# Token-list rows of 64 bytes, and the transposes of the third unit of 256 tokens two parts later in TensorE's order

## The chip, the cores and the metric

The kernel runs on one core of one Trainium2 chip. Its engines are TensorE (PE, with its weight loads shown apart as PEld), VectorE (DVE), ScalarE (ACT), GpSimd (POOL) and SyncE (SP), and 16 DMA engines serve the core. POOL and SP issue DMAs: SP's go out on the queue that the trace calls hardware_dynamic, POOL's indirect ones on software_dynamic. The metric is device time in microseconds, the median of several executions. One further execution was profiled, and all rows of the trace come from that one.

## What is computed

Three stages follow one another on 2 x 768 tokens of 512 values in float32.

```
x   = attention(q, k, v) with a mask: query and key in the same nearest-centroid cluster
e   = argmax(x @ w_gate + bias[modality]);  g = softmax weight of expert e
y   = g * (relu(x @ w1[e]) @ w2[e])            # one of 8 experts per token
h   = y @ w_in;  out = (max(h,0) + log1p(exp(-|h|))) @ w_out
```

The expert stage is the one of interest: each token goes to one of eight experts, so tokens have to be sorted by expert, gathered, multiplied by that expert's weights, and put back.

## The kernel before, in words

**Stages.** Attention of batch 0, then of batch 1 (to about 300 us), the experts, and the dense pair of matmuls at the end. The work of the expert stage starts for batch 0 while attention of batch 1 still runs. The order in which the code issues instructions is the order on each engine: there is a manual schedule and no scheduler behind it. DMAs of SP and POOL also go out in the order of the code on these engines.

**The token list.** After routing, each token has a row number in a list in device memory, `token_list`: 1536 rows per expert and some rows for surplus, 13312 rows in all. `scatter_list` (L592 to 599, the DMA is issued on L589) writes the tokens' numbers into it: for each batch six indirect DMAs of 128 rows, issued by POOL, with a small memset `spacer` (L588) ahead of each. A row is one 4-byte word. `init_list` fills the list once, early in attention: POOL sets the tile `empty` (L1035), and SP stores it. The tokens' own rows `x_rows` (2 KB each) are stored apart.

**Units.** Tokens are worked on in units. F0 and F1 are full units of 256 tokens of batch 0, chosen early. F2 to F4 are full units whose expert and place in the list come from tables made once all tokens are routed; M1 to M3 are small units (32, 128 and 32 tokens); F5 is a late one. For a unit of the tables
- `u_list` (L752 to 766): SP reads the place from a register load (L757) and loads the token numbers, `it<-token_list` (L765 or L762),
- `u_gather` (L768 to 779): POOL clips them (`gi`, L772) and gathers the rows of x by them, one indirect DMA per 128 tokens (`xg<-x_rows,gi`, L776),
- `u_xpose` (L793 to 798, with `to_T`): PE transposes 128 tokens in four matmuls into the one PSUM bank `misc` (L785), ACT copies them to `xh` (L788), and DVE subtracts to get the low half `xl` (L790),
- `l1_part` (L818) multiplies by the first weights in four groups for each half of the hidden values, s=0 and s=1, and `l2_part` (L843) by the second: for each half 24 matmuls, 12 into the bank of j=0 and 12 into that of j=1,
- `u_out` copies and scatters the result, `y_rows<-ysb,it`.

**Weights.** They come as chunks of 512 KB: SP loads `raw` (L730), ACT casts the high half `wh` (L740), and DVE or POOL subtracts the low half `wl` (L741). A matmul group takes `wh`, `wl` and `wh` again.

**The order.** A list `seq` of parts (unit, layer, half) sets what PE does. Tables made ahead of it say what is issued with each part: `before` (the transposes ahead of a part), `gathers`, `loads`, `todo` (the splits). F2 and M1 are the first two units that take their places from the tables: both list loads and all three gathers of these two are issued with the last layer-1 part of F1, behind the list's second six scatters. On POOL the subtraction of one weight chunk, wl_3783, stands behind the three gathers. It is the low half of F1's first chunk of second weights, so it belongs to the second matmul of F1's layer 2.

Of the kernel before, what the change touches and what calls it, by code (L numbers as in the profile page):

```python
# [12 lines left out]
U32 = mybir.dt.uint32  # L13
# [19 lines left out]
def body(ctx, tc, qT, kT, vP, cen, mod, wg, bias, w1, w2, win, wout, out):  # L33
    nc = tc.nc
# [4 lines left out]
    NT = S // 128  # L39
# [2 lines left out]
    DUMMY = E * CAP  # L42
    LATE = DUMMY + 256 * NF
    LROWS = LATE + 256
    NM = N // 256
    CW = 1024
    pe, dve, act, pool, sp = nc.tensor, nc.vector, nc.scalar, nc.gpsimd, nc.sync

    xd = nc.dram_tensor("x_rows", (N, DM), F32, kind="Internal").ap()
    yd = nc.dram_tensor("y_rows", (N, DM), F32, kind="Internal").ap()  # L50
    lst = nc.dram_tensor("token_list", (LROWS, 1), U32, kind="Internal").ap()
    wf = nc.dram_tensor("w_rows", (16, 128, 1024), F32, kind="Internal").ap()

    const = ctx.enter_context(tc.tile_pool(name="const", bufs=1))
# [10 lines left out]
    def ctile(shape, dt, name):  # L65
        return const.tile(shape, dt, name=name)
# [2 lines left out]
    desc8 = ctile([128, E], F32, "desc8")  # L69
    tri = ctile([128, 128], BF16, "tri")  # L70
    ones = ctile([128, 128], BF16, "ones")
    tokid = ctile([128, 2 * NT], U32, "tokid")
    gate = ctile([128, 2 * NT], F32, "gate")
    lbias = ctile([128, 2 * NT, E], F32, "lbias")
    lacc = [ctile([128, NT, E], F32, f"lacc{b}") for b in range(2)]
# [29 lines left out]
    def setup_late():  # L105
        pool.iota(desc8, pattern=[[-1, E]], base=E, channel_multiplier=0, allow_small_or_imprecise_dtypes=True)
        pool.iota(e_off, pattern=[[CAP, E]], base=0, channel_multiplier=0, allow_small_or_imprecise_dtypes=True)
        pool.iota(tokid, pattern=[[128, 2 * NT]], base=0, channel_multiplier=1)
        pool.memset(e_row, 0.0)
        pool.iota(e_row[0:1], pattern=[[0, NT + 1], [CAP, E]], base=0, channel_multiplier=0, allow_small_or_imprecise_dtypes=True)  # L110
        pool.memset(e_row[0:1, NT, :], 0.0)
        pool.iota(iota_u, pattern=[[1, 16]], base=0, channel_multiplier=0, allow_small_or_imprecise_dtypes=True)
        pool.iota(u_fix, pattern=[[0, 3], [1, NK]], base=0, channel_multiplier=0, allow_small_or_imprecise_dtypes=True)
        for i, b in enumerate((128, 32, 0)):
            pool.iota(thr[:, i, :], pattern=[[256, 6]], base=b, channel_multiplier=0, allow_small_or_imprecise_dtypes=True)
        dve.tensor_reduce(out=fold, in_=ident.rearrange("p (g t) -> p t g", g=4), axis=AX.X, op=ALU.add)
        pool.iota(x_row, pattern=[[CAP, 9]], base=0, channel_multiplier=0, allow_small_or_imprecise_dtypes=True)
        pool.memset(ones, 1.0)
        pool.memset(tri, 1.0)
        pool.affine_select(  # L120
            out=tri, in_=tri, pattern=[[1, 128]], base=0, channel_multiplier=-1,
            compare_op=ALU.is_gt, fill=0.0,
        )
        pool.memset(pre9, 1.0)
        pool.affine_select(
            out=pre9, in_=pre9, pattern=[[1, 9], [-1, E]], base=0, channel_multiplier=0,
            compare_op=ALU.is_gt, fill=0.0,
        )
        pool.memset(drow, 0.0)
        pool.memset(nunit, 0.0)  # L130
        pool.memset(d_row, 0.0)
# [462 lines left out]
    def scatter_list(b, idx):  # L594
        for t in range(NT):
            scatter(
                "list", out=lst, out_offset=bass.IndirectOffsetOnAxis(ap=idx[:, t:t + 1], axis=0),
                in_=tokid[:, b * NT + t:b * NT + t + 1], in_offset=None,
            )

    def pick_early(cnt):
# [152 lines left out]
    def u_list(u, eng=sp):  # L754
        b = u["base"]
        if not isinstance(b, int):
            b = eng.value_load(b, min_val=0, max_val=DUMMY + 256 * (NF - 1))  # L757
        it = small.tile([128, 2], U32, tag="it", name="it", bufs=NF + NHU + NTU + 3)
        gi = small.tile([128, 2], U32, tag="gi", name="gi", bufs=NF + NHU + NTU + 3)
        with nc.allow_non_contiguous_dma(reason="token lists are columns of words"):  # L760
            if u["tiny"]:
                eng.dma_start(out=it[:32, 0:1], in_=lst[bass.ds(b, 32)])  # L762
            else:
                n = u["n"]
                eng.dma_start(out=it[:, :n], in_=lst[bass.ds(b, 128 * n)].rearrange("(j p) o -> p (j o)", p=128))  # L765
        u["it"], u["gi"] = it, gi

    def u_gather(u):  # L768
# [23 lines left out]
    def u_xpose(u, j):  # L792
        if j == 0:  # L793
            w = 32 if u["tiny"] else 128 * u["n"]
            u["xh"] = u["xtp"].tile([128, 4, w], F32 if u["tiny"] else F32R, tag="xh", name="xh")
            u["xl"] = None if u["tiny"] else u["xtp"].tile([128, 4, w], F32R, tag="xl", name="xl")
        to_T(u["xg"][j], u["xh"], u["xl"], j, 32 if u["tiny"] else 128)
# [47 lines left out]
    def u_out(u, j, free=True):  # L845
        y = u["yp"].tile([128, DM], F32, tag="ysb", name="ysb")
        if j == 0:
            act.copy(y, u["y"][j])
        else:
            dve.tensor_copy(y, u["y"][j])  # L850
        kw = dict(
            out=yd, out_offset=bass.IndirectOffsetOnAxis(ap=u["it"][:, j:j + 1], axis=0),
            in_=y, in_offset=None, bounds_check=N - 1, oob_is_err=False,
        )
        if free:
            scatter("late" if u["late"] else "y", **kw)
        else:
            pool.indirect_dma_start(**kw)
# [85 lines left out]
    with tc.manual_schedule():  # L944
# [83 lines left out]
                    busy.add(g0 + k)  # L1028
            after.setdefault(g0 + 4, []).append((cv_store, (j,)))

        e_t = p_1.tile([128, LROWS // 128], U32, name="empty")

        def init_list():
            setup_late()
# [235 lines left out]
        def at_part(table, n, x):  # L1270
            table.setdefault(n, []).append(x)

        for (kd, k, layer, s), n in pos.items():
            if layer == 1 and s == 0 and n > 1:
                v = (F if kd == "F" else M)[k]
                back = [x for x in range(2, n) if seq[x][0] == "F" or seq[x][2] < 3]
                for j in range(v["n"]):
                    at_part(before, back[j - v["n"]], (v, j))
                if v not in early_ and v is not U1:
                    at_part(gathers, [x for x in back if seq[x][0] == "F"][-3 if kd == "F" else -4], v)  # L1280
        nsplit = [0]
# [132 lines left out]
        for n in range(2, end):  # L1414
            kind, i, layer, s = seq[n]
            if n == x_at:
                extra_units()
            u = (F if kind == "F" else M)[i]
            if n == x_at + 2:
                for k in range(3):  # L1420
                    y_load(k)
                y_gate(0)
                y_gate(1)

            for v, j in before.get(n, ()):
                u_xpose(v, j)
            if kind == "F" and layer == 1:
                for f in range(4):
                    l1_part(u, s, f)
            elif kind == "F" and i == LF:  # L1430
                if s == 0:
                    for j in range(2):
                        l2_part(u, 0, [j])
                        if j:
                            y_T(0, 1)
                        l2_part(u, 1, [j])
                        if not j:
                            y_T(0, 0)
                        splits(n + j)
                        u_out(u, j)  # L1440
            elif kind == "F":
                l2_part(u, s)
            elif layer == 2:
                s_l2(u)
            elif layer == 4:
                t_out(u)
            elif layer == 1:
                (t_l1 if u["tiny"] else h_l1)(u)
            if kind == "F" and layer == 1 and s == 0:
                l1_evac(u, 0)  # L1450
            if n == 5:
                route_gate(1)
                count_extra()
            if n > 3 and us:
                u_list(us.pop(0))
            for v in gathers.get(n, ()):
                u_gather(v)
            if not (kind == "F" and i == LF and layer == 2):
                splits(n)
            for k in loads[n]:  # L1460
                load(k)
            if n == 2:
                for v in range(2):
                    u_list(us.pop(0))
            if kind == "F" and layer == 1 and s == 1:
                l1_evac(u, 1)
            elif kind == "F" and layer == 2 and s == 1 and i < LF:
                for j in range(2):
                    u_out(u, j)
            elif kind == "M" and layer == 1:  # L1470
                h_evac(u)
            elif kind == "M" and layer == 2:
                (t_part if u["tiny"] else lambda u: u_out(u, 0))(u)
            elif kind == "M" and layer == 3:
                h_xp(u)
# [145 lines left out]
```

## Time and profile before

| | |
|---|---|
| median of 3 executions | 756.45 us (753.99 to 763.52) |
| the profiled execution | 757.96 us, of which the span of the core is 756.2 us |
| mean granted clock of TensorE, as a share of full speed | 0.986 |
| PE busy | 706.8 us (93% of the span) |
| DVE, ACT, POOL busy | 455.2, 392.6, 157.1 us |
| DMA | 99.29 MB, 8254 of 38683 packets under 512 B |

Times in the rows are microseconds from the start of the span. A timeline row has its start, its busy time, the engine, the line, the operation, out<-in, sizes and the count of like instructions in one row; brackets hold the idle time before it and what ended that. A busy time of one matmul holds its passage through the array; matmuls overlap, so the pace is read from their starts. In a row of --waits "x <- y: a, n, b" means that x waited for y, a us in total, n times, b the longest. "us to landing" of a DMA is the time from its issue to the end of its last packet.

### The profile page before, as it was taken

To read this page: it belongs to the slowest core of one execution; us is meant where nothing else is said; L and a number is where in the kernel's file an instruction comes from. 1 tells how busy PE (TensorE), PEld (TensorE's weight loads), DVE (VectorE), ACT (ScalarE), POOL (GpSimd) and SP (SyncE) were. 2 spreads that over 40 slices of the span, in tenths; PEclk is the share of its full clock that TensorE was granted. 3 is DMA by queue.
4 is the path that set the end of the run, shared out by engine and by line. 5 is a ranking of instruction groups with operands and counts; after the bars stand their busy time and mean duration, and the time that the engine had idled before them with its cause. 6 is when DMAs were issued, how large, how long until landed. Compare 5 with 4: busy or idle time off the path is not lost. (4 is left out here: it accounts for less than half of the span.)

```text
span 756.2 us, 11743 instructions
## 1 busy us (share of the span) xinstructions
PE 706.8 (93%) x4498; PEld 565.8 (75%) x4498; DVE 455.2 (60%) x668; ACT 392.6 (52%) x635; POOL 157.1 (21%) x172
## 2 busy tenths in 40 slices
PE   4898999899899989968999999998999999999998
PEld 2665665665566656857888879998899899899887
DVE  5898997899799975934546554686323324223220
ACT  3777886888678865524556553643332322323310
POOL 4301210111411205624542430261000000000000
PEclk9999999999999999997999999999999999999999
DMA  4317355453645344879868974500010000000000
GB/s 135 105 28 269 118 172 186 159 173 117 203 114 210 122 164 150 184 183 384 317 211 293 394 276 154 181 1 29 1 43 15 29 15 29 1 1 29 1 29 28
DMA packets 38683, 99.29 MB, mean 131 GB/s; under 512 B 8254, under 2 KB 15614, under 8 KB 36576
## 3 DMA queue, kind: packets, MB, share of 16 engines
q1 hardware_dynamic: 35888, 91.42, 36.4%
q0 software_dynamic: 2592, 6.69, 2.5%
q8 instruction: 36, 0.59, 0.3%
q10 hardware_dynamic: 144, 0.39, 0.2%
q14 instruction: 23, 0.19, 0.1%
HBM read 79.13 MB, written 18.28 MB: 129 GB/s over the span
## 5 line engine op out<-in xcount | busy, mean ns | idle before, releaser
L1500 DVE SCALAR_TENSOR_TENSOR sp<-g,sp 128x1024 f32<-128x1024 f32 x24 | 29.4, 1224 | 148.8 <-ACT sp L1499 148.8
L1489 PE MATMUL g<-xh,wh 128*128 128x256 f32 x384 | 108.7, 283 | 0.0
L1489 PE MATMUL g<-xh,wl 128*128 128x256 f32 x384 | 107.9, 281 | 0.0
L1489 PE MATMUL g<-xl,wh 128*128 128x256 f32 x384 | 107.9, 281 | 0.0
L330 ACT ACTIVATE P<-S,nm 128x768 f32<-128x768 f32 x96 | 87.0, 907 | 37.0 <-DVE nm L321 34.5
L343 PE MATMUL Tp<-ident,P 128*128 128x128 f32 x576 | 85.5, 282 | 14.0 <-ACT PT L348 8.9
L321 DVE TENSOR_REDUCE nm<-S 128x1 f32<-128x768 f32 x96 | 90.7, 946 | 8.9 <-PE S L319 8.6
L1497 ACT ACTIVATE sp<-g 128x1024 f32<-128x1024 f32 x24 | 24.6, 1027 | 136.6 <-PE g L1489 126.7
L343 PEld LDWEIGHTS Tp<-ident,P 128*128 128x128 f32 x576 | 68.9, 144 | 27.0 <-ACT PT L348 14.5
L741 POOL TENSOR_TENSOR wl<-raw,wh 128x1024 fp32r<-128x1024 f32 x22 | 54.1, 2467 | 135.2 <-ACT wh L740 128.2
L355 PE MATMUL av<-PT,v 128*64 128x384 f32 x384 | 79.8, 511 | 0.0
L741 DVE TENSOR_TENSOR wl<-raw,wh 128x1024 fp32r<-128x1024 f32 x50 | 65.2, 1344 | 14.7 <-ACT wh L740 14.7
L740 ACT CAST wh<-raw 128x1024 fp32r<-128x1024 f32 x69 | 68.9, 1050 | 9.6 <-DMA raw<-in_w 6.8
L1489 PEld LDWEIGHTS g<-xl,wh 128*128 128x128 f32 x384 | 73.0, 190 | 0.5
L1489 PEld LDWEIGHTS g<-xh,wh 128*128 128x128 f32 x384 | 72.8, 190 | 0.5
L1489 PEld LDWEIGHTS g<-xh,wl 128*128 128x128 f32 x384 | 73.0, 190 | 0.0
L348 ACT COPY PT<-Tp 128x384 f32<-128x384 f32 x144 | 64.1, 483 | 16.4 <-PE Tp L343 15.7
L1524 PE MATMUL o<-wh,gT 128*128 128x512 f32 x216 | 69.8, 394 | 0.0
L304 PEld LDWEIGHTS S<-kA,qA 128*128 128x128 f32 x192 | 30.1, 197 | 50.2 <-issue 14.5
L304 PE MATMUL S<-kA,qA 128*128 128x384 f32 x192 | 61.1, 401 | 3.8 <-ACT P L330 3.5
L843 PE MATMUL y<-wh,hT 128*128 128x512 f32 x192 | 64.5, 407 | 0.0
L818 PE MATMUL h<-xh,wh 128*128 128x256 f32 x192 | 55.1, 287 | 0.5 <-DVEq L1346 0.5
(284 smaller groups left out, 1402.3 us busy)
## 6 DMA issues: line engine op xcount, KB each, us to landing
raw<-in_w SPq DMA_DIRECT2D x56, 512.0 KB, 7.4
words<-in_win SPq DMA_DIRECT2D x8, 1024.0 KB, 7.0
w_rows<-cvt SPq DMA_DIRECT2D x16, 512.0 KB, 3.0
words<-in_wout SPq DMA_DIRECT2D x8, 1024.0 KB, 7.5
whole<-in_w SPq DMA_DIRECT2D x16, 512.0 KB, 5.6
raw<-w_rows SPq DMA_DIRECT2D x16, 512.0 KB, 5.4
rawq<-in_qT SPq DMA_DIRECT2D x8, 384.0 KB, 3.3
v<-in_vP SPq DMA_DIRECT2D x8, 384.0 KB, 5.2
```

What stands on the lines that cost most here:

```text
L304: pe.matmul(ps[:, i, :HS], qA[:, t * 128:t * 128 + 128], kA[:, i * HS:(i + 1) * HS], start=True, stop=False)
L321: dve.tensor_reduce(out=nm_t[g], in_=ps[:, :, :HS], axis=AX.XY, op=ALU.max, negate=True)
L330: act.activation(out=P_t[g], in_=S_t.pop(g)[:, :, :HS], func=AF.Exp, bias=nm_t.pop(g), scale=1.0, accum_out=sums[h][:, t:t + 1],)
L343: pe.transpose(ps[:, j, :], P[:, i, j * 128:(j + 1) * 128], ident)
L348: act.copy(dst, ps)
L355: pe.matmul(av_t[h][64 * a:64 * a + 64, :], vt[p][:, kt, 64 * i:64 * i + 64], PT[h][:, kt, a * HS:(a + 1) * HS], start=(kt == 0), stop=(kt ...
L740: cp(self.hi, self.raw)
L741: eng.tensor_tensor(out=self.lo, in0=self.raw, in1=self.hi.bitcast(F32), op=ALU.subtract)
L818: pe.matmul(o, a, b[:, kt, :], start=(n == 0 and f % 2 == 0), stop=(n == 11), skip_group_check=True)
L843: pe.matmul(u["y"][j], x, y, start=(kt == 0 and i == 0), stop=(kt == 7 and i == 2))
L1489: pe.matmul(o, a, b[:, kt, :], start=(n == 0 and f % 2 == 0), stop=(n == 11), skip_group_check=True)
L1524: pe.matmul(ys[u][j], x[:, a:a + 128], y, start=(kt == 0 and i == 0), stop=(kt == 15 and i == 2))
```

## The change

It has two parts. The list's rows become 16 words (64 bytes) wide. The tile of token numbers, `tokid`, holds each number 16 times, a scatter writes all 16, and the list loads take word 0 of each row; the tile `empty` and its store grow to 16 times their size (52 KB to 832 KB). And the two sets of transposes of F2 move in the order: those of j=0 from ahead of the first half of F1's layer 2 to ahead of its second half, those of j=1 from ahead of that second half to its middle, behind its 12 matmuls of j=0.

```diff
+    LW = 16
-    lst = nc.dram_tensor("token_list", (LROWS, 1), U32, kind="Internal").ap()
+    lst = nc.dram_tensor("token_list", (LROWS, LW), U32, kind="Internal").ap()
-    tokid = ctile([128, 2 * NT], U32, "tokid")
+    tokid = ctile([128, 2 * NT, LW], U32, "tokid")
-        pool.iota(tokid, pattern=[[128, 2 * NT]], base=0, channel_multiplier=1)
+        pool.iota(tokid, pattern=[[128, 2 * NT], [0, LW]], base=0, channel_multiplier=1)
...
-                in_=tokid[:, b * NT + t:b * NT + t + 1], in_offset=None,
+                in_=tokid[:, b * NT + t, :], in_offset=None,
...
-                eng.dma_start(out=it[:32, 0:1], in_=lst[bass.ds(b, 32)])
+                eng.dma_start(out=it[:32, 0:1], in_=lst[bass.ds(b, 32), 0:1])
...
-                eng.dma_start(out=it[:, :n], in_=lst[bass.ds(b, 128 * n)].rearrange("(j p) o -> p (j o)", p=128))
+                eng.dma_start(out=it[:, :n], in_=lst[bass.ds(b, 128 * n), 0:1].rearrange("(j p) o -> p (j o)", p=128))
...
-        e_t = p_1.tile([128, LROWS // 128], U32, name="empty")
+        e_t = p_1.tile([128, LROWS // 128 * LW], U32, name="empty")
...
-                for j in range(v["n"]):
-                    at_part(before, back[j - v["n"]], (v, j))
+                if v is F[2]:
+                    at_part(before, back[-1], (v, 0))
+                else:
+                    for j in range(v["n"]):
+                        at_part(before, back[j - v["n"]], (v, j))
...
+            elif kind == "F" and i == 1 and s == 1:
+                l2_part(u, s, [0])
+                u_xpose(F[2], 1)
+                l2_part(u, s, [1])
```

**TensorE at the start of F1's layer 2.** Names end in the program's buffer numbers: xg_3775 and xg_3777 are F2's gathered rows (j=0 and j=1), hT_3867 and hT_3988 are F1's two halves of hidden values, and the two y are its results. Brackets hold the semaphores that an instruction waits for. Before:

```order
L818 MATMUL h_3886<-xh_3646,wl_3690 128x256
L785 MATMUL misc_3993<-ident_85,xg_3775 128x128 [waits DMASW0_49,PE_49]
L785 MATMUL misc_3993<-ident_85,xg_3775 128x128 x3
L843 MATMUL y_4000<-wh_3782,hT_3867 128x512 [waits Activation_49]
L843 MATMUL y_4000<-wl_3783,hT_3867 128x512 [waits Pool_49]
L843 MATMUL y_4000<-wh_3782,hT_3867 128x512 [waits DVE_49]
L843 MATMUL y_4001<-wh_3782,hT_3867 128x512
```

Now:

```order
L819 MATMUL h_3886<-xh_3646,wl_3690 128x256
L844 MATMUL y_3991<-wh_3782,hT_3867 128x512 [waits Activation_49]
L844 MATMUL y_3991<-wl_3783,hT_3867 128x512 [waits Pool_49]
L844 MATMUL y_3991<-wh_3782,hT_3867 128x512 [waits DVE_49]
L844 MATMUL y_3992<-wh_3782,hT_3867 128x512
```

The four transposes that wait for the gather no longer stand ahead of the first half's 24 matmuls. The second of these matmuls waits for POOL in both orders.

**TensorE at the second half of F1's layer 2.** Before, the transposes of j=1 stood here:

```order
L843 MATMUL y_4001<-wh_3786,hT_3867 128x512
L785 MATMUL misc_4065<-ident_85,xg_3777 128x128 [waits DMASW1_49,DVE_49]
L785 MATMUL misc_4065<-ident_85,xg_3777 128x128 x3
L843 MATMUL y_4000<-wh_3790,hT_3988 128x512 [waits Activation_49]
L843 MATMUL y_4000<-wl_3791,hT_3988 128x512
```

Now those of j=0 stand here, and those of j=1 twelve matmuls on:

```order
L844 MATMUL y_3992<-wh_3786,hT_3867 128x512
L786 MATMUL misc_4058<-ident_85,xg_3775 128x128 [waits DMASW0_49,PE_49]
L786 MATMUL misc_4058<-ident_85,xg_3775 128x128 x3
L844 MATMUL y_3991<-wh_3790,hT_3988 128x512 [waits Activation_49]
L844 MATMUL y_3991<-wl_3791,hT_3988 128x512
...
L844 MATMUL y_3991<-wh_3882,hT_3988 128x512
L786 MATMUL misc_4077<-ident_85,xg_3777 128x128 [waits DMASW1_49,DVE_49]
L786 MATMUL misc_4077<-ident_85,xg_3777 128x128 x3
L844 MATMUL y_3992<-wh_3790,hT_3988 128x512
L844 MATMUL y_3992<-wl_3791,hT_3988 128x512
```

The second half's matmuls ran through both banks chunk by chunk; now all 12 of the first bank come ahead of the 12 of the second.

**ScalarE at the same place.** The copies `xh` of the transposes, before:

```order
L824 ACTIVATE hT_3988<-h_3886 128x1024 [waits PE_49,Activation_49]
L788 CAST xh_3991<-misc_3993 128x4x128 [waits PE_49,Activation_49]
L740 CAST wh_4038<-raw_3704 128x1024 [waits DMAHW5_49]
L740 CAST wh_4042<-raw_3798 128x1024 [waits DMAHW4_49,Pool_49]
L740 CAST wh_4046<-raw_3800 128x1024 [waits DMAHW5_49,Pool_49]
L788 CAST xh_3991<-misc_4065 128x4x128 [waits PE_49]
```

Now:

```order
L825 ACTIVATE hT_3988<-h_3886 128x1024 [waits PE_49,Activation_49]
L741 CAST wh_4029<-raw_3704 128x1024 [waits DMAHW5_49]
L741 CAST wh_4033<-raw_3798 128x1024 [waits DMAHW4_49,Pool_49]
L741 CAST wh_4037<-raw_3800 128x1024 [waits DMAHW5_49,Pool_49]
L789 CAST xh_4056<-misc_4058 128x4x128 [waits PE_49,Activation_49]
L789 CAST xh_4056<-misc_4077 128x4x128 [waits PE_49]
```

Both copies now stand behind three weight casts; on DVE both `xl` likewise stand behind two subtractions of weights. POOL's order is the same as before: scatters of the list, `gi`, three gathers, then wl_3783.

## Rows read from the trace of the kernel before

**Rows 1.** Waits of PE by cause, 320 to 460 us (columns as above).

```profile
PE misc L785 <- DMA xg<-x_rows,gi: 10.2, 1, 10.2
PE h L818 <- DVEq L1346: 0.5, 1, 0.5
```

**Rows 2.** Timeline of PE around F1's layer 2.

```profile
332.59 0.28 PE L818 MATMUL h<-xh,wl 128*128 128x256 f32 x1
343.02 1.08 PE L785 MATMUL misc<-ident,xg 128*128 128x128 f32 x4 [10.15 <-DMA xg<-x_rows,gi]
...
351.31 0.60 PE L785 MATMUL misc<-ident,xg 128*128 128x128 f32 x4
351.67 0.48 PE L843 MATMUL y<-wh,hT 128*128 128x512 f32 x1
...
357.31 0.43 PE L785 MATMUL misc<-ident,xg 32*128 32x32 f32 x4
```

**Rows 3.** Windows: stretch, length, busy and count by engine, PEclk, DMA share, GB/s.

```profile
343.10:351.30 8.20, 8.20 (x28) 6.67 (x29) 4.40 (x3) 3.42 (x4) 3.69 (x4) 0.70 0.94 348
351.30:357.30 6.00, 6.00 (x29) 4.76 (x27) 3.05 (x3) 3.08 (x4) 0.00 (x0) 1.00 1.03 412
```

**Rows 4.** Timeline of POOL, third, fifth and sixth scatter of the second list to wl_3783.

```profile
312.61 0.97 POOL L589 DMA_INDIRECT token_list<-tokid,ridx  x1 [0.21 <-issue]
...
315.16 4.34 POOL L589 DMA_INDIRECT token_list<-tokid,ridx  x1 [0.22 <-issue]
...
319.81 2.56 POOL L589 DMA_INDIRECT token_list<-tokid,ridx  x1 [0.21 <-issue]
335.15 0.21 POOL L772 TENSOR_SCALAR gi<-it 128x2 uint32<-128x2 uint32 x1 [12.78 <-DMA it<-token_list]
...
339.71 2.36 POOL L741 TENSOR_TENSOR wl<-raw,wh 128x1024 fp32r<-128x1024 f32 x1
```

**Rows 5.** Timeline of SP's DMA issues in the same stretch.

```profile
333.02 0.38 SPq L765 DMA_DIRECT2D it<-token_list  x1
...
335.92 2.08 SPq L730 DMA_DIRECT2D raw<-in_w  x4
```

**Rows 6.** DMA issues of the window 320:322: median us to landing.

```profile
token_list<-tokid,ridx POOLq DMA_INDIRECT x1, 13.0
```

**Rows 7.** DMA queue in 310:312: packets, MB, share of 16 engines.

```profile
q1 hardware_dynamic: 137, 0.47, 57.8%
```

**Rows 8.** The same queue in 314:316.

```profile
q1 hardware_dynamic: 16, 0.07, 223.0%
```

**Rows 9.** DMA issues of the whole span: KB each, median us to landing.

```profile
xg<-x_rows,gi POOLq DMA_INDIRECT x15, 6.1
...
token_list<-tokid,ridx POOLq DMA_INDIRECT x12, 12.2
...
token_list<-empty SPq DMA_DIRECT2D x1, 52.0 KB, 1.5
...
y_rows<-yq,it POOLq DMA_INDIRECT x2, 3.9
```

**Rows 10.** Timeline of DVE beside the fifth scatter.

```profile
315.18 3.47 DVE L741 TENSOR_TENSOR wl<-raw,wh 128x1024 fp32r<-128x1024 f32 x3
```

**Rows 11.** DMA issues of the window 336:340.

```profile
raw<-in_w SPq DMA_DIRECT2D x4, 512.0 KB, 7.9
```

**Rows 12.** Timeline of DVE, the weight splits used soonest.

```profile
407.55 3.49 DVE L741 TENSOR_TENSOR wl<-raw,wh 128x1024 fp32r<-128x1024 f32 x3
```

**Rows 13.** Timeline of PE, first use of the first of these splits.

```profile
416.98 0.40 PE L843 MATMUL y<-wl,hT 128*128 128x512 f32 x1
```

**Rows 14.** Timeline of POOL early, behind the memset of `empty` (L1035).

```profile
42.14 0.83 POOL L278 TENSOR_SCALAR kA<-rawk 64x768 fp32r<-64x768 f32 x1 [10.85 <-PE S L304]
```

**Rows 15.** Longest waits of PE, 198 to 240 us.

```profile
PE Tp L343 <- ACT PT L348: 2.5, 2, 2.1
```

**Rows 16.** Windows: 205 to 210 us, inside that stretch.

```profile
205.00:210.00 5.00, 4.88 (x27) 3.67 (x25) 4.90 (x10) 5.00 (x13) 2.62 (x4) 0.69 0.25 23
```

## The prediction, made before the changed kernel was run

> **What bounds the kernel now.** PE is busy for 706.8 of 756.2 us, so I read the waits of PE first. From 320 to 460 us, where the expert units run, PE waits once for long: 10.2 us, the transposes of F2 for their gathered rows; nearly everything else of that stretch is matmuls back to back [rows 1]. The timeline shows the place: layer 1 of F1 is over at 332.87 (332.59 + 0.28), and the transposes of j=0 start at 343.02, after 10.15 idle [rows 2]. From there to the transposes of j=1 (351.31) it is 8.29 us, from these to M1's (357.31) only 6.00, for the same four transposes and 24 matmuls. The windows tell why: a granted clock of 0.70 in the first stretch, 1.00 in the second [rows 3]. So the wait costs 10.15 + (8.29 - 6.00) = **12.44 us**, and no more than that can be won here. At full clock 24 matmuls take 357.31 - 351.67 = 5.64 us, 0.235 each, and the transposes 0.36.
>
> What PE waits for is a chain. SP loads F2's token numbers at 333.02 [rows 5], 0.21 after the list's last scatter has landed (319.81 + 13.0 = 332.81) [rows 4, 6]; POOL has idled 12.78 when they arrive, clips, issues three gathers, and then makes wl_3783, from 339.71 to 342.07 [rows 4]. From SP's load to the end of wl_3783 it is 342.07 - 333.02 = **9.05 us**.
>
> The scatter's 13.0 us are the odd link. While its neighbours are in flight, SP's packets of 4 KB stick: in 310 to 312 us 137 packets take 57.8% of 16 engines x 2 us, 0.135 us each; in 314 to 316 us sixteen packets take 223%, 4.5 us each, with 0.07 MB moved [rows 7, 8]. The median of all twelve list scatters is 12.2 us, though 2-KB rows are gathered in 6.1 and scattered (y_rows<-yq) in 3.9 [rows 9]. Scatters of 512 bytes in all are thus slower than those of 256 KB. What sets them apart is that their 4-byte rows lie side by side in device memory.
>
> **The move of the transposes** takes them from ahead of the first half's 24 matmuls. Alone it hides little, because the second of these matmuls waits for wl_3783, which POOL still makes behind the gathers. PE would start the first at 332.87, and reach the second at 333.10. If the list is no earlier, it waits until 342.07; 23 matmuls at the low clock follow (7.55/24 each, 7.24), then both sets of transposes and the second half (0.36 + 6.00): M1's transposes at 355.67, **1.6 us** earlier than 357.31.
>
> Splitting the second half by banks keeps its 24 matmuls: nothing. The move also puts ACT's xh behind three weight casts and DVE's xl behind two subtractions. The raws of these casts are issued 2.9 us of the list load (335.92 - 333.02) [rows 5], land 7.9 later [rows 11]; the last one needed is the second of four, 0.5 on (2.08/4), and its cast is priced as a subtraction of the same size, 1.2 (3.49/3) [rows 12]: list load + 12.5. PE comes to the transposes of j=0 at list load + 9.05 + 23 x 0.235 = + 14.5 or later. Cover: 2.0 us. Beyond it, PE would be late only at j=1, which needs the bank that xl must free first and stands 12 matmuls (2.8 us) on.
>
> **The 64-byte rows** leave the count of scatters, gathers and list loads as it was. Each scatter writes 8 KB instead of 0.5 KB. Call L the landing of the last scatter after its issue, then the list load goes at 319.81 + L + 0.21, and wl_3783 ends 9.05 later. No row shows 64-byte rows, so L has two bounds. The upper one that I take for rows that no longer stick is the gather's 6.1, the lower the store of 52 KB, 1.5 [rows 9]; to either comes what POOL's own issue was longer than the 0.97 of an undisturbed one, 2.56 - 0.97 = 1.6 [rows 4], if that stays. I use 3.9 + 1.6 = **5.5**, because y_rows<-yq is the one other scatter by POOL, and from above 7.7, from below 3.1. With 5.5: list load at 325.5, wl_3783 done at 334.6, PE waits 1.5 us at the second matmul. A wait that short may or may not lower the clock for the first half: 0 to 23 x (0.315 - 0.235) = 1.8 us; I take 1.0. M1's transposes are then at 334.6 + 5.4 + 6.36 + 1.0 = 347.3, **10.0 us** earlier. With 7.7 and the whole clock cost it is 6.9; with 4.1 or less, nothing waits, and all 12.4 come.
>
> POOL's own delay has two readings. Its fifth scatter takes 4.34 us, from 315.16 to 319.50, and three subtractions run on DVE from 315.18 to 318.65 [rows 4, 10]. The stuck packets of the same stretch fit as well: an issue that finds no room. If 64-byte rows end the sticking, this reading would end the sixth issue near 317.4, 5 us earlier, and PE would not wait at all: the 12.4. The Trainium skill ("SBUF — State Buffer", section "SBUF: two separate sides") says that GpSimd cannot write a DMA's descriptors while DVE runs a two-port mode. By that rule the long issues stay, and the sum is the 10.0; this trace shows the coincidence and not the cause.
>
> **The rest.** `empty` grows 16 times: a memset of 1664 words in a partition, by the 2.36 us of POOL's 1024-word subtraction at most 3.8 us, where POOL then idles 10.85 [rows 4, 14]; its store of 832 KB needs some 2.3 us at the 348 to 412 GB/s of rows 3, against 1.5 for 52 KB [rows 9]. Both are early, nobody reads the list before routing, and I cost them at nothing; if a load of that stretch is pushed behind the store, up to 2.3 us come on top. `tokid` (192 words instead of 12) adds at most 0.4 by the same price. A list load reads the same 4-byte pieces, from rows 64 bytes apart, and needs one more register operation on SP: nothing to 0.4 us.
>
> What is late next: the weight split used soonest afterwards is done at about 408.8 (the first of three in 3.49 us from 407.55) and used at 416.98: 8.2 us of room [rows 12, 13]. PE comes 10.0 earlier, but so do the loads, which stand on SP behind the list load: 7.5 earlier. If they did not move at all, 1.8 us would be given back.
>
> **Sum.** 757.96 - 10.0 = 748.0 for an execution like the profiled one. That one is 1.5 us over the median, so against the median: 756.45 - 10.0 = **746.5 us**. About 2% (15.1 us) is what a measurement of this kernel can tell from no change; the whole wait is worth less than that.
>
> **Rivals.**
> *A, the forecast:* 744.0 to 749.6 us (gains 12.4 to 6.9). Chance 0.70.
> *B, the rows don't help:* the list still takes 13.0 us, PE's wait moves from the gather to POOL's wl_3783, and 1.6 us are left: 754.8. For it: 8254 packets of the kernel are under 512 B and 64-byte rows stay among them; against it, that most of these small packets delay nothing that the waits show. Chance 0.17. The Trainium skill ("DMA: Bandwidth & Descriptors", section "Specifications") asks for 512 bytes at least and says that below this the DMA engine reads, modifies and writes; by this rule alone 64 bytes are as slow as 4, which is B. No run here shows a row width between.
> *C, slower:* if each row is a transaction whose cost grows with its bytes, the second list's backlog lengthens. It decides from a landing later than 334.4 on (list load + 9.05 + 13.6 past 357.31). Twice the 20.2 us from the third scatter (312.61) [rows 4] to 332.81 would be a landing at 353.0, wl_3783 at 362.3, and 18.6 us lost: 775.0; over 2% slower from 349.5 on. Against it: the 6.1 and 3.9 us of 2-KB rows. Chance 0.05.
> *D, more:* the first list's scatters fall into attention of batch 1, where PE waits 2.5 us at one place [rows 15] and runs at 0.69 for 5 us, which costs 4.88 x 0.31 = 1.5 [rows 16]. If that too comes from packets stuck behind the list, 4.0 us come on top of 10.0 to 12.4: 740.0 to 742.4. Chance 0.08, since PE waits there for ACT, and a DMA is only behind it.
>
> **Range and chances.** A alone is 744 to 750. Reaching for a median that moves by a microsecond or two from run to run (753.99 to 763.52 shown) and for B, 742.5 to 756 leaves out D, C, a quarter of B and a little of A: 0.08 + 0.05 + 0.04 + 0.02. Faster by over 2% (under 741.3): half of D, 0.04, and 0.04 of A by scatter of the median: 0.08. Slower by over 2%: most of C, 0.04. Within 2%: 0.88.
>
> **What would show it.** In A the window 314 to 316 us has SP's packets at tenths of a microsecond, the last list scatter lands within 4 to 8 us, F2's list load goes near 325.5, PE has a short wait or none at the second y matmul, named as POOL wl, and the first half's clock is nearer 1.00. In B the landing stays near 13, and PE waits some 9 us for POOL wl. In C the landing is past 334. The idle time of POOL before the first gi tells how far the list moved; the busy time of the fifth and sixth scatter, which reading of POOL's delay holds. The forecast would be wrong if the sticking were not the 4-byte rows' doing, or if ACT's xh came later than the weights and PE waited for misc at j=1.

## The result, and the profile after

The change takes 747.39 us in the median of 4 executions (744.6 to 748.49), against 757.98 for the kernel before on the same chip (4 executions, 753.99 to 763.52). The ratio is 0.9846, with a 95% interval of 0.9808 to 0.9884: 8.8 to 14.6 us less. Forecast were 746.5 us and 10.0 us less, in a range of 742.5 to 756. Under 2%, this counts as no change by the bound that the prediction named, but the interval lies clear of 1. The 746.5 stood on a median of three executions of before, 756.45; with a fourth it is 757.98, 1.5 higher, so the gain by medians is 10.6.

The profiled execution of the change has a span of 746.8 us, 9.4 less than the one before. Its waits of PE from 305 to 460 us, to be held against [rows 1] (x <- y: us, times, longest):

```profile
PE y L844 <- POOL spacer L589: 1.3, 1, 1.3
PE h L819 <- DVEq L1350: 0.5, 1, 0.5
PE misc L786 <- DVE xl L791: 0.4, 1, 0.4
```

The wait of 10.2 us for the gather is gone. In its place stand 1.3 us at the second matmul, for POOL. The profile names spacer, the next instruction on POOL; what the matmul waits for is wl_3783, which ends at 332.77 + 2.38 = 335.15 below, just ahead of the matmul at 335.21. PE's timeline, against [rows 2]:

```profile
333.35 0.28 PE L819 MATMUL h<-xh,wl 128*128 128x256 f32 x1
333.46 0.40 PE L844 MATMUL y<-wh,hT 128*128 128x512 f32 x1
335.21 0.51 PE L844 MATMUL y<-wl,hT 128*128 128x512 f32 x1 [1.35 <-POOL spacer L589]
...
340.61 0.60 PE L786 MATMUL misc<-ident,xg 128*128 128x128 f32 x4
343.81 0.60 PE L786 MATMUL misc<-ident,xg 128*128 128x128 f32 x4
347.09 0.43 PE L786 MATMUL misc<-ident,xg 32*128 32x32 f32 x4
```

The 23 matmuls from 335.21 to 340.61 take 5.40 us, 0.235 each. That is full clock, and the window says the same, against 0.70 in [rows 3]:

```profile
335.20:340.60 5.40, 5.39 (x23) 4.38 (x24) 5.36 (x5) 2.49 (x3) 4.58 (x4) 1.00 1.03 374
```

POOL's timeline answers to [rows 4], SP's list load to [rows 5]:

```profile
315.92 4.34 POOL L590 DMA_INDIRECT token_list<-tokid,ridx  x1 [0.22 <-issue]
...
320.57 2.56 POOL L590 DMA_INDIRECT token_list<-tokid,ridx  x1 [0.23 <-issue]
327.20 0.21 POOL L773 TENSOR_SCALAR gi<-it 128x2 uint32<-128x2 uint32 x1 [4.07 <-DMA it<-token_list]
...
332.77 2.38 POOL L742 TENSOR_TENSOR wl<-raw,wh 128x1024 fp32r<-128x1024 f32 x1
```

```profile
325.43 0.39 SPq L766 DMA_DIRECT2D it<-token_list  x1
```

POOL's idle time ahead of the first gi fell from 12.78 to 4.07 us. The last scatter, issued at 320.57, lands after 4.6 us instead of the 13.0 of [rows 6] (window 320.5 to 321, us to landing):

```profile
token_list<-tokid,ridx POOLq DMA_INDIRECT x1, 4.6
```

And SP's packets no longer stick. In the window 314.5 to 316.5, 3.7 us behind the list's first scatter (that of [rows 8] begins 4.0 behind it), 78 of them take 59.3% of 16 x 2 us, 0.24 us each instead of 4.5:

```profile
q1 hardware_dynamic: 78, 0.32, 59.3%
```

**A measure for what follows.** Executions of one kernel differ by some 10 us, so small steps are read from one stage of the profile: from the start of F1's last layer-1 matmul to M1's transposes. Before it is 357.31 - 332.59 = 24.72 us, in the change 347.09 - 333.35 = 13.74. The stage gave **10.98 us**. The span gained 9.4, because in this execution the stage began 0.76 us later and the rest after M1's transposes took 0.82 longer. The stage has its own scatter: a second profiled execution of the change shows

```profile
333.77 0.28 PE L819 MATMUL h<-xh,wl 128*128 128x256 f32 x1
347.02 0.43 PE L786 MATMUL misc<-ident,xg 32*128 32x32 f32 x4
```

which is 13.25 us, 0.49 less than the first, with 0.9 us of waiting for POOL instead of 1.3. Every other kernel below has one profiled execution, so differences of about half a microsecond in the stage say nothing.

### The profile page after: what moved, and what is told of

Same layout as the page of the kernel before. It is cut to its first block, busy times and chain, and to the rows that moved or that the text cites. A ratio compares the mean times of both kernels' runs of the same rounds, so it can differ in the third digit from the quotient of the medians.

```text
span 746.8 us, 11746 instructions
## 1 busy us (share of the span) xinstructions
PE 703.2 (94%) x4498; PEld 562.5 (75%) x4498; DVE 457.7 (61%) x668; ACT 392.3 (53%) x635; POOL 160.7 (22%) x172
```

## The experiments

The theory: rows that are neighbours in device memory slow each other's writes, and what is in flight beside them; the late list then holds up gather and wl_3783 together; where PE waits for them is a matter of the order. The rivals: the moved transposes are what gains, or 64 bytes are too few and another width is needed.

**Only the rows.** The change without the two edits that move the transposes (LW = 16 stays).

> 64-byte rows, the transposes of F2 at their old places. Theory (the rows move the whole chain, the order only places the rest of the wait): the list load goes near 325.4 and the gather lands some 10.2 us later, at 335.7; PE, free at about 333.6 in the profile of the change, waits 2 us for it at the transposes instead of 10.2, wl_3783 is ready by then; gain 8.5 to 10.4 us against before, within 2 us of the whole change. Rival (the move of the transposes is what gains): PE goes on waiting for the gather for over 6 us and the gain is under 5 us.

Measured: 747.68 us, ratio 0.9883 (0.9828 to 0.9937), stage 14.51 us, 10.2 less than before. PE's longest wait:

```profile
PE misc L786 <- DMA xg<-x_rows,gi: 2.2, 1, 2.2
```

The stage runs between these two:

```profile
331.27 0.28 PE L819 MATMUL h<-xh,wl 128*128 128x256 f32 x1
345.78 0.43 PE L786 MATMUL misc<-ident,xg 32*128 32x32 f32 x4
```

The rows alone bring nearly all. The rival that the move gains is out: with the old order PE waits 2.2 us for the gather, with the new one 1.3 for POOL.

**Only the move.**

```diff
-    LW = 16
+    LW = 1
```

> Only the move of the transposes, list rows of 4 bytes. Theory: the list lands as late as before (13 us for the last scatter), PE waits some 9 us at the second matmul of F1's layer 2 for wl_3783 on POOL, gain 1.6 us (0 to 3). Rival (the move hides the gather): gain over 5 us and no wait on POOL.

Measured: 759.28 us, ratio 1.0013 (0.9981 to 1.0046): no gain can be seen; stage 24.27 us, 0.45 less, which is within the scatter of the stage. The wait and the window of the 23 matmuls behind it:

```profile
PE y L844 <- POOL spacer L589: 9.2, 1, 9.2
```

```profile
345.80:353.80 8.00, 7.94 (x23) 6.30 (x24) 3.87 (x2) 2.09 (x2) 4.77 (x6) 0.64 0.95 357
```

As expected the wait has only changed its name. In this execution the gain is smaller than 1.6, because the wait was 0.3 longer and the matmuls behind it ran at 0.64 instead of 0.70: 8.0 us instead of the 7.24 that I had put in.

**The move with wl_3783 ahead of the gathers on POOL**, rows of 4 bytes.

```diff
-    LW = 16
+    LW = 1
...
+            if n == 3:
+                splits(n)
             for v in gathers.get(n, ()):
                 u_gather(v)
-            if not (kind == "F" and i == LF and layer == 2):
+            if n != 3 and not (kind == "F" and i == LF and layer == 2):
                 splits(n)
```

> List rows of 4 bytes, the transposes moved, and on POOL wl_3783 ahead of the gathers of F2 and M1 instead of behind them. Theory: wl_3783 is made while POOL waits for the list, done near 325.7, so PE runs the first half of layer 2 at once and waits only at the transposes of j=0 for the gather: 342.9 minus 338.5 = 4.4 us plus up to 1.5 us of lower clock; gain 6.5 to 8 us. Rival (POOL's order is not what holds the second matmul): gain as for the move alone, 1.6 us.

Measured: 755.32 us in the median of 10, ratio 0.9960 (0.9929 to 0.9991), 0.7 to 5.4 us less; stage 17.97 us, 6.75 less. In the profile wl_3783 stands where the theory puts it (POOL), and PE first waits at the transposes:

```profile
318.18 2.56 POOL L590 DMA_INDIRECT token_list<-tokid,ridx  x1 [0.22 <-issue]
320.77 2.40 POOL L742 TENSOR_TENSOR wl<-raw,wh 128x1024 fp32r<-128x1024 f32 x1
```

```profile
340.82 0.63 PE L786 MATMUL misc<-ident,xg 128*128 128x128 f32 x4 [4.07 <-DMA xg<-x_rows,gi]
```

The mechanism holds in the profiled execution. Of its 6.75 us, 1.3 come from a list that was sooner in this execution: the list load follows the last scatter's issue by 330.07 - 318.18 = 11.89 us, against 13.2 before.

```profile
330.07 0.38 SPq L766 DMA_DIRECT2D it<-token_list  x1
```

The medians show 4 us, less than the 6.5 to 8 that were expected; the profiled execution was one of the three fastest of ten. What the others did stays open, since the landing of the list is known only where there is a trace.

**The change with wl_3783 ahead of the gathers**: the same edit of POOL's order, with LW = 16.

> The change, and on POOL wl_3783 ahead of the gathers. Theory: the 1.35 us that PE still waits at the second matmul go, nothing takes their place since the gathers are issued at the same time (POOL idles 4.07 us ahead of them); 0.5 to 1.5 us less than the change, gain against before 11 to 12.4 us. Rival (the wait comes back at the transposes of j=0 or for xh behind ACT's casts): no faster than the change.

Measured: 746.25 us, ratio 0.9851 (0.9803 to 0.9899), stage 13.87: no better than the change. The rival came true in its outcome, though the wait is for DVE's xl at j=1:

```profile
PE misc L786 <- DVE xl L791: 2.0, 2, 1.6
```

DVE's timeline shows why. Its first subtraction takes 2.59 us and ends at 340.68, 1.1 us after one that POOL makes from 337.19 to 339.59; the second follows, and then xl, which ends at 342.42:

```profile
338.09 2.59 DVE L742 TENSOR_TENSOR wl<-raw,wh 128x1024 fp32r<-128x1024 f32 x1 [0.66 <-ACT wh L741]
```

PE has the transposes of j=0 done at 337.9, and starts those of j=1 at 342.47, once xl has freed the bank.

**The width of the rows.** Three versions of the change, with LW = 2, 4 and 8 in place of 16. In the order in which they ran:

> The change with list rows of 32 bytes (8 words). If a stretch of 64 bytes of device memory shared by several rows is what slows their writes, two rows still share one, and the last scatter lands late, between the 4.6 us of 64-byte rows and the 13.0 of 4-byte rows, some 6 to 10 us; PE waits for wl_3783 by as much longer than 1.3 us. If only the bytes of one row matter (half of them, half of the effect), about the same. If 32 bytes are a whole unit already, it lands in 4 to 5 us as with 64.

> The change with list rows of 16 bytes (4 words). Shared stretch of 64 bytes: four rows share one, the last scatter lands in 9 to 12 us, and SP's packets of 4 KB still take over 1 us beside it. If the unit is 16 bytes or less: 4 to 5 us.

> The change with list rows of 8 bytes. 16 bytes landed in some 5.9 us and 4 bytes in 13.0. If the writes that share a stretch disturb each other the more of them there are, the last scatter lands between, in 7 to 10 us, and PE waits 4 to 6 us for wl_3783. If only the single word is slow: under 6 us.

PE's wait for POOL in each, 8, 16 and 32 bytes in this order:

```profile
PE y L844 <- POOL spacer L589: 5.2, 1, 5.2
```

```profile
PE y L844 <- POOL spacer L589: 3.0, 1, 3.0
```

```profile
PE y L844 <- POOL spacer L589: 1.3, 1, 1.3
```

The table adds the time from the issue of the last scatter to SP's list load, and the time of SP's packets of 4 KB in 2 us at the first weight load behind the scatters (share x 32 us / packets; a packet counts in full where it begins, so a share can pass 100%):

| bytes of a row | last scatter's issue to the list load | us of one 4-KB packet | stage |
|---|---|---|---|
| 4 (the kernel before) | 13.2 | 4.46 (223.0%, 16) | 24.72 |
| 8 | 7.8 | 3.22 (161.1%, 16) | 19.77 |
| 16 | 6.1 | 1.47 (105.7%, 23) | 15.36 |
| 32 | 5.4 | 0.24 (65.0%, 86) | 13.73 |
| 64 (the change) | 4.9 | 0.24 (59.3%, 78) | 13.74 |

The single executions took 755.20, 751.91 and 747.77 us for 8, 16 and 32 bytes. The expectation for 16 bytes failed in one half: packets took over 1 us, but the scatter landed in some 6 us, not 9 to 12. That for 8 bytes came true with 5.2 us of waiting. Of the three outcomes named for 32 bytes the last came: 32 do as well as 64. The effect shrinks with each doubling and is gone by 32. Each row of the table stands on one profiled execution; for 4 and 64 bytes others agree: a packet took 4.60 us in the move alone (16 at 229.8%, from 317.01 us on) and 0.25 in the rows alone (69 at 54.4%, from 312.95 us on).

**4 bytes, 64 bytes apart.** The rows stay 64 bytes apart, but a scatter writes only their first word.

```diff
+        idxw = small.tile([128, NT], U32, tag="idxw", name="idxw")
+        pool.tensor_scalar(out=idxw, in0=idx, scalar1=float(LW), scalar2=None, op0=ALU.mult)
...
-                "list", out=lst, out_offset=bass.IndirectOffsetOnAxis(ap=idx[:, t:t + 1], axis=0),
-                in_=tokid[:, b * NT + t, :], in_offset=None,
+                "list", out=lst.rearrange("r (w o) -> (r w) o", o=1),
+                out_offset=bass.IndirectOffsetOnAxis(ap=idxw[:, t:t + 1], axis=0),
+                in_=tokid[:, b * NT + t, 0:1], in_offset=None,
```

> The change, but a scatter writes only word 0 of each row of 64 bytes (4 bytes, 64 bytes apart; the row numbers are multiplied by 16 on POOL first, about 0.2 us). Theory (neighbours disturb each other): spacing alone ends the sticking, the last scatter lands in 4 to 6 us and the time is that of the change within 2 us. Rival (a write under a full unit is slow by itself, whoever its neighbour is): the landing stays at 12 to 13 us, PE waits about 9 us for wl_3783, and the time is that of the move alone, some 10 us above the change.

Measured: 748.82 us, ratio 0.9840 (0.9791 to 0.9890), stage 13.86; PE's longest wait is 1.4 us, not the 9 of the rival:

```profile
PE y L847 <- POOL spacer L589: 1.4, 1, 1.4
```

SP's packets in the 2 us from its next weight load on take 0.29 us each:

```profile
q1 hardware_dynamic: 81, 0.33, 73.1%
```

POOL's last two scatters, and SP's list load:

```profile
321.01 2.56 POOL L590 DMA_INDIRECT token_list<-tokid,idxw  x1 [0.22 <-issue]
...
323.87 0.97 POOL L590 DMA_INDIRECT token_list<-tokid,idxw  x1 [0.22 <-issue]
```

```profile
326.37 0.39 SPq L769 DMA_DIRECT2D it<-token_list  x1
```

The load follows the last scatter's issue by 2.5 us. (The multiplication put the scatters one place later beside DVE, so here the fourth and fifth are the long ones.) **Spacing does it, not size**: the same 4-byte writes are harmless when nothing lies beside them. This is the experiment that tells the theory from its rival. One thing it does not part: with the spacing, the list also spreads over a longer stretch of memory (52 KB before, 832 KB here and in the change). Whether it is rows that touch, or the short stretch as such, was not tried.

**Three of DVE's subtractions moved to POOL**, behind its scatters, in the change.

```diff
-                split(k, pool if n == 1 or nsplit[0] % 5 == 0 and n > 2 else dve)
+                split(k, pool if n <= 2 or nsplit[0] % 5 == 0 and n > 2 else dve)
```

> The change, with the three weight subtractions that run on DVE beside the fifth scatter moved to POOL, behind its six scatters. Theory (DVE's subtractions hold up POOL's issue): the fifth and sixth scatter take about 1 us each instead of 4.34 and 2.56, the last one lands near 2 us after its issue, the list load goes some 4 to 5 us earlier; POOL is then busy with its subtractions until about 325.5, gathers at once, and has wl_3783 done near 332.5, before PE comes (333.4): no wait of PE over 0.5 us from 320 to 460, 1 to 2 us less than the change. Rival (stuck packets held POOL up, or another cause): the fifth scatter still takes over 3 us, the gathers wait for POOL's subtractions and PE waits as long as or longer than in the change.

Measured: 747.14 us, ratio 0.9831 (0.9793 to 0.9868), stage 13.73. POOL's timeline:

```profile
315.17 0.97 POOL L590 DMA_INDIRECT token_list<-tokid,ridx  x1 [0.22 <-issue]
316.45 0.97 POOL L590 DMA_INDIRECT token_list<-tokid,ridx  x1 [0.23 <-issue]
317.44 7.13 POOL L742 TENSOR_TENSOR wl<-raw,wh 128x1024 fp32r<-128x1024 f32 x3
```

The fifth and sixth scatter take 0.97 us: it was DVE's subtractions that held their issue. The gain that I expected from it did not come, and SP's waits name the reason:

```profile
SPq L731 <- POOL wl L742: 4.8, 1, 4.8
```

POOL frees the raw buffers later than DVE did, SP stands 4.8 us ahead of a weight load, and the list load behind it goes at 323.20, among the weight loads; its words reach POOL at 327.18, 4.0 us later; in the change it is 327.20, 1.8 us after the load. DVE, too, pays for its neighbour. A subtraction that begins while POOL's three run takes 5.85 us, where [rows 10] has three in 3.47; it ends at 325.65, 1.1 us after the last of POOL's (317.44 + 7.13 = 324.57):

```profile
319.80 5.85 DVE L742 TENSOR_TENSOR wl<-raw,wh 128x1024 fp32r<-128x1024 f32 x1 [1.20 <-ACT wh L741]
```

**The casts held back.** wl_3783 ahead of the gathers, and the splits and loads of F1's layer 2, first half, behind both transposes of F2.

```diff
...
             elif kind == "F" and i == 1 and s == 1:
                 l2_part(u, s, [0])
                 u_xpose(F[2], 1)
+                splits(n - 1)
+                for k in loads[n - 1]:
+                    load(k)
                 l2_part(u, s, [1])
             elif kind == "F":
                 l2_part(u, s)
+                if i == 1:
+                    u_xpose(F[2], 0)
...
+            held = kind == "F" and i == 1 and layer == 2 and s == 0
+            if n != 3 and not held and not (kind == "F" and i == LF and layer == 2):
+                splits(n)
-            for k in loads[n]:
+            for k in loads[n] if not held else ():
                 load(k)
```

> The change with wl_3783 ahead of the gathers on POOL, and with the weight splits and loads of F1's layer 2, first half, held back behind both transposes of F2, so that ACT makes xh and DVE xl before these weights; TensorE's order as in the change. Theory (both remaining waits of PE, for wl_3783 and for xl behind the casts, are places in a queue): PE waits under 0.5 us in this stretch except the 0.5 us on DVEq, some 1.3 us less than the change, all 12.4 us of before won; the splits held back have 12 us of room or more. Rival (the raws that are now loaded later are missed by M1 or F2): a new wait of PE for a wl between 345 and 400.

> The change itself again, beside the version with the held casts: 746 to 749 us, 10 to 12 us under before; 0 to 2 us above the held casts.

Measured, on one chip and beside the same kernel before (758.73): 747.98 us, ratio 0.9857 (0.9814 to 0.9899), for the held casts, 747.23 us, ratio 0.9833 (0.9781 to 0.9884), for the change. PE's waits from 305 to 460 us with the held casts:

```profile
PE h L819 <- DVEq L1348: 0.5, 1, 0.5
PE misc L786 <- DVE lbe L563: 0.2, 1, 0.2
```

The stage is 12.12 us, 12.60 less than before: all of it, and no new wait behind. That is 1.1 us less than the profile of the change on this chip (13.25) and 1.6 less than the first one (13.74). The runs do not resolve this; the medians even stand the other way. No version was measurably faster than the change.

## Why the prediction was right

- **The bound, 12.44 us.** It holds: the stage with no wait left gave 12.60, 0.16 over the bound and inside the stage's scatter, and the change 10.98.
- **The chain behind the list.** Forecast was a list load at 325.5 and 9.05 us from it to the end of wl_3783; it was 325.43 and 335.15 - 325.43 = 9.72. That the load matches is in part luck: the landing was 0.9 us shorter than put in, and the scatter was issued 0.76 later in this execution. The 0.7 more lie ahead of M1's gather, whose gi took 1.23 us instead of 0.22. A subtraction of DVE stands beside it, and gi ends 0.08 after that:

```profile
330.21 1.22 DVE L742 TENSOR_TENSOR wl<-raw,wh 128x1024 fp32r<-128x1024 f32 x1
330.28 1.23 POOL L773 TENSOR_SCALAR gi<-it 32x1 uint32<-32x1 uint32 x1
```

Since the execution ran 0.76 later up to here, PE still waited only 1.35 us, for 1.5 forecast; the second execution of the change waited 0.9.
- **The landing, L.** Taken as 5.5 between 3.1 and 7.7, measured 4.6. Without the 1.6 of POOL's own issue that is 3.0, between the 1.5 of the store and the 3.9 of y_rows<-yq, and nearer to the second, which the prediction had used. That was luck. Its reason, that y_rows<-yq is the one other scatter by POOL, does not hold: it moves the 32 rows of a small unit (64 KB, not 256), and the trace of before has 13 scatters of 128 such rows, which took longer:

```profile
y_rows<-ysb,it POOLq DMA_INDIRECT x13, 6.0
```

With 6.0 in place of 3.9, L would have been 7.6 and the forecast 7 to 8 us of gain, where 10.6 were measured.

- **The clock after a short wait** was the term furthest off: 1.0 us put in, none measured, the granted clock being 1.00 behind a wait of 1.35 and also behind the 2.2 of the rows alone. It is most of the 1.0 by which the stage beat the forecast.
- **The move.** Alone it was worth 0.45 us in the stage, which is within its scatter, and nothing in the runs, for 1.6 forecast. Beside the rows it gains 14.51 - 13.74 = 0.8 us in one profile of the change, 1.3 in the other, and nothing that the medians show (747.68 without it).
- **ACT's cover, 2.0 us.** The third cast ended at 338.64, PE came at 340.61. The 2.0 were there. With wl_3783 first they were used up: the third cast ended at 339.00, PE came to j=0 at 337.55, and the wait came back at j=1, where the prediction had put it, though through DVE, whose subtraction ended 1.1 us behind POOL's.
- **POOL's long issues.** Of the two readings, DVE's subtractions are right: with them gone the issues fall from 4.34 and 2.56 to 0.97, and with the sticking gone, but the subtractions there, they stay. The rule of a two-port mode that the prediction took for this does not cover them. The Trainium skill ("SBUF — State Buffer", section "Who interferes with whom") gives a subtraction of two tensors no two-port mode, and reports a probe in which such an instruction did not hold up a DMA. Here it held up the issue, and the measured 4.34 against 0.97 decides; which step of the issue is held, the runs do not show.
- **B, 64 bytes too few.** It is out: 32 bytes sufficed, and so did 4 with room around them. The Trainium skill ("DMA: Bandwidth & Descriptors", section "Specifications") gives 512 bytes as the least for full rate; the rate of small writes was not measured here, so no run bears on that.
- **C** fell with the landing of 4.6.
- **D, more from the first list.** Its scatters land sooner too (the median of all twelve is 3.8 us, for 12.2), but PE waits there as before, against [rows 15]:

```profile
PE Tp L344 <- ACT PT L349: 2.7, 2, 2.3
```

The low clock of [rows 16] does not follow the list either: over 205 to 210 us it is 1.00 in this profile of the change, 0.57 in the second and 0.66 in the rows alone.

- **The small costs.** The memset of `empty` took 1.48 us, for at most 3.8, its store 3.3, for 2.3, and no engine's wait names it. For the extra step in a list load (nothing to 0.4 us) the prediction named no row; the load of M1's list follows F2's by 1.19 us instead of 1.15.

## What to carry to other kernels

When many small writes go to neighbouring words of device memory, look at what else is in flight: the price stands in the packets of other DMAs and in the landing (4.5 and 13.0 us), not in the small packets' own times (in the window of [rows 8], 32 of them took 1.2% of 16 x 2 us, 0.01 us each). Give each record room before you make it large. When a wait goes by a change of order, first look for what else the waiting engine needs from behind the same event; here the next matmul's weights stood in the same queue, and the move by itself was worth nothing that the runs show.

## What the runs showed of the hardware that I had not expected

- 4-byte rows side by side make 4-KB packets of another queue take 4.5 us instead of 0.14 to 0.29; 8-byte rows 3.2, 16-byte rows 1.5, 32-byte rows 0.24. The runs show that the distance between the rows does it; what unit of memory close rows share, they do not show.
- DVE's subtractions and POOL's work hold each other up. A subtraction on DVE that begins while POOL's are running ends 1.1 us after them, about its own length (3.47/3), in two kernels (340.68 behind 339.59, 325.65 behind 324.57), and a scatter's issue on POOL ends 0.85 us after DVE's group (319.50 behind 318.65) [rows 4, 10].
- The clock behind a wait in this stage was 1.00 after 1.35, 2.2 and 3.0 us (the change, the rows alone, 16 bytes), 0.64 over 4.8 us after 4.1 (wl_3783 first, rows of 4 bytes), 0.69 over 7.5 after 5.2 (8 bytes), and 0.64 to 0.70 after 9.2 to 10.2. The length of the wait alone does not decide it: in attention it was 0.69 behind 2.1 us before [rows 15, 16], and 1.00 behind 2.3 in the change.
